# Soft-capped attention and soft mixture of experts on one core: score tiles, chain places and joined tanhs replanned

## The chip, the cores and the metric

The kernel runs on one core of one Trainium2 chip. The metric is device time in microseconds. Before the change the median of three runs is 281.64 us (281.38 to 281.78).

The core's engines work on instruction queues of their own and wait for each other through semaphores: PE (TensorE, matrix products and transposes), DVE (VectorE), ACT (ScalarE), POOL (GpSimd) and SP (SyncE, here only transfers). Each queue is worked off strictly in the order in which the program puts it down.

## The reference

Attention with soft-capped scores over 8 x 12 heads, 448 tokens, head size 64, then a soft mixture of 8 experts with 4 slots each:

```python
scores = scale * np.matmul(q, k.transpose(0, 1, 3, 2))
scores = cap * np.tanh(scores / cap)                       # cap = 30
attn = np.exp(scores - np.max(scores, axis=-1, keepdims=True))
attn = attn / (np.sum(attn, axis=-1, keepdims=True) + 1e-09)
attn_out = np.matmul(attn, v)

logits = x @ phi                                           # x: attn_out as 3584 x 768
d = softmax of logits over the tokens                      # written out in the reference
slot_input = d.T @ x
h = np.maximum(slot_input[e] @ w1[e], 0.0); slot_out[e] = h @ w2[e]
c = softmax of logits over the slots                       # written out in the reference
out = c @ slot_out
```

## The kernel before

**Tiles and chunks.** Two heads make a pair: 48 pairs, two of which share one load (a quad, `Q`, 24 of them, three to a batch element). A score tile is 64 + 64 keys of two heads by 448 queries, that is 128 x 448; a pair has 7 of them, so there are 336. They are worked in 56 chunks of 6 (`CH`), each chunk in two halves of 3 (`CS`). One half of scores fills three PSUM banks.

**What happens to a chunk `j`.**
- PE makes the scores of a half (`qk_chunk`, products on L349).
- ACT takes the tanh of each half out of PSUM (`tanh_chunk`, L366). In a chunk of the tuple `JOINED` one instruction takes both halves (L362), from a six-bank tile (`board`) that replaces the two three-bank tiles from the first joined chunk to the last.
- The exponential follows. `exp_chunk(j)` is one ACT instruction (L374) over the tiles that ACT keeps. The first tiles of the chunks in `SHARED` (chunk: (tiles, buffer)) go to DVE instead, as a *chain* of seven steps (`poly_exp`, L602 to L609) that builds 2^x with a polynomial and integer bit work: steps 0, 1, 3 and 6 are scalar steps (one input tensor), steps 2, 4 and 5 tensor steps (two inputs). All chains share one pair of buffers, `xf` and `xp`.
- ACT runs chunk `j`'s exp between the tanhs of chunk `j + 1` and chunk `j + 2`; the exps of chunks 0 and 1 stand right behind their own tanhs, so chunk 2 has none behind its tanh.
- Two chunks after a pair's last tile, PE multiplies its weights with the values (`pv_first`, `pv_tail`, `pv_rest`; L627) into one PSUM bank (`pv`, the only one of its kind). DVE takes the reciprocal of the row sums (L634, in `norm`) and multiplies (L637, tile `xq`). Only then may the next pair's products go into the bank.

**The order is written out by hand.** The main loop runs over the chunks, and `run(j, slot)` calls, between its fixed steps, what a table `aux` holds for that slot. The slots of a chunk are, in order, `0`, `m` (between the two tanhs), `e`, `a`, `b`, `r`, `c`, `d`; `<` and `>` put a call ahead of or behind the others of a slot. `r` is special: where a pair is finished in the chunk, its calls stand between the reciprocal and the multiplication of `norm`. The dictionary `POLY` says for each (chunk, slot) which steps of which chains go there. `WHEN` places the loads, the transposes of k and q (copied out of PSUM by DVE on L281), the transposes of x (`x_transp`, L689), the logits (`logits`), the slot sums (`slot_sums`, DVE's `slacc` on L778) and so on; `spare`, `fill` and `busy` put filler products on PE.

**Order within a chunk.** Behind the tanhs and the exp, PE's queue has `pv_first`, the calls of `a`, `pv_tail`, the next chunk's first half of scores, the calls of `b`, `pv_rest`, the calls of `c`, the second half of scores, the calls of `d`. In a joined chunk the first half of scores stands behind `pv_rest` instead.

**The end.** In chunk 55 the last pairs are finished outside the loop's pattern (`TAILSEQ`): products of pair 45 in the `pv` bank, then those of pair 46 (`pvm`) and pair 47 (`pvl`) in banks of their own, transposes and logits between them. Behind the attention come the slot sums of the last batch element, the two expert layers (`layer1`, `layer2`) and the output.

Of the kernel before, what the change touches and what calls it, by code (L numbers as in the profile page):

```python
# [37 lines left out]
def kernel(  # L38
# [23 lines left out]
    NQB = H // 4  # L62
# [313 lines left out]
    def exp_chunk(j):  # L376
# [4 lines left out]
    JOINED = (10, 14, 17, 21, 24, 28, 29, 31, 35, 38, 42, 45, 49)  # L381
    SHARED = {1: (2, 0), 3: (3, 0), 4: (3, 0), 6: (2, 0), 7: (3, 0), 9: (3, 0), 11: (3, 0), 12: (3, 0), 14: (3, 0), 16: (3, 0), 18: (3, 0), 19: (3, 0), 21: (3, 0), 23: (3, 0), 25: (3, 0), 26: (3, 0), 28: (3, 0), 30: (3, 0), 32: (3, 0), 33: (3, 0), 35: (3, 0), 37: (3, 0), 39: (3, 0), 40: (3, 0), 42: (3, 0), 44: (3, 0), 46: (3, 0), 47: (2, 0), 48: (2, 0), 49: (3, 0), 51: (2, 0), 52: (1, 0), 53: (3, 0), 54: (1, 0)}
    POLY = {(1, 'm'): ((1, 0),),
            (1, 'e'): ((1, 1),),
            (1, '>a'): ((1, 2),),
            (1, '>b'): ((1, 3),),
            (1, '>d'): ((1, 4),),
            (2, 'r'): ((1, 5),),
            (3, 'e'): ((3, 0),),
            (3, '<a'): ((3, 1), (1, 6)),  # L390
            (3, '<b'): ((3, 2),),
            (3, '>c'): ((3, 3),),
            (4, '<a'): ((3, 4),),
            (4, '>a'): ((3, 5),),
            (4, '<c'): ((4, 0),),
            (5, 'e'): ((4, 1), (3, 6)),
            (5, '<a'): ((4, 2),),
            (5, '>b'): ((4, 3),),
            (5, '>c'): ((4, 4),),
            (6, 'e'): ((6, 0), (4, 5), (6, 1)),  # L400
            (6, '<a'): ((4, 6),),
            (6, '>d'): ((6, 2),),
            (7, 'm'): ((6, 3),),
            (7, 'e'): ((7, 0),),
            (7, '>a'): ((6, 4),),
            (7, '<b'): ((6, 5),),
            (7, '<d'): ((7, 1),),
            (8, '0'): ((7, 2), (7, 3)),
            (8, '>b'): ((6, 6), (7, 4)),
            (8, '>c'): ((7, 5),),  # L410
            (9, 'm'): ((9, 0),),
            (9, '<a'): ((7, 6),),
            (9, '>b'): ((9, 1),),
            (9, '>d'): ((9, 2),),
            (10, 'e'): ((9, 3),),
            (10, '>b'): ((9, 4),),
            (10, '>d'): ((9, 5),),
            (11, 'e'): ((11, 0),),
            (11, '<a'): ((9, 6),),
            (11, '>a'): ((11, 1),),  # L420
            (11, '>b'): ((11, 2),),
            (11, '<c'): ((11, 3),),
            (11, '>c'): ((11, 4),),
            (12, '<a'): ((12, 0),),
            (12, '<b'): ((11, 5),),
            (12, '<c'): ((12, 1),),
            (12, '>d'): ((11, 6),),
            (13, '<b'): ((12, 2),),
            (13, '>b'): ((12, 3),),
            (13, '>c'): ((12, 4),),  # L430
            (13, '>d'): ((12, 5),),
            (14, '<a'): ((14, 0), (12, 6), (14, 1)),
            (14, '<d'): ((14, 2), (14, 3)),
            (15, '>a'): ((14, 4),),
            (15, '>d'): ((14, 5),),
            (16, 'm'): ((14, 6),),
            (16, 'e'): ((16, 0),),
            (16, '<b'): ((16, 1),),
            (16, '>d'): ((16, 2),),
            (17, 'm'): ((16, 3),),  # L440
            (17, '<a'): ((16, 4),),
            (17, '>d'): ((16, 5),),
            (18, 'e'): ((18, 0),),
            (18, '>a'): ((16, 6), (18, 1)),
            (18, '>b'): ((18, 2),),
            (19, '0'): ((18, 3), (18, 4)),
            (19, 'e'): ((18, 5),),
            (19, '<a'): ((19, 0),),
            (19, '<c'): ((18, 6),),
            (19, '>c'): ((19, 1), (19, 2)),  # L450
            (20, '>b'): ((19, 3),),
            (20, '>d'): ((19, 4),),
            (21, '>a'): ((19, 5), (19, 6)),
            (21, '<b'): ((21, 0), (21, 1)),
            (21, '>c'): ((21, 2),),
            (21, '<d'): ((21, 3),),
            (22, '>b'): ((21, 4),),
            (22, '<d'): ((21, 5),),
            (23, 'm'): ((21, 6),),
            (23, '<a'): ((23, 0),),  # L460
            (23, '>a'): ((23, 1),),
            (23, '>d'): ((23, 2),),
            (24, 'e'): ((23, 3), (23, 4)),
            (24, '>d'): ((23, 5),),
            (25, 'm'): ((23, 6),),
            (25, '<a'): ((25, 0), (25, 1)),
            (25, '>b'): ((25, 2),),
            (25, '<c'): ((25, 3),),
            (25, '>d'): ((25, 4),),
            (26, '0'): ((25, 5),),  # L470
            (26, '<b'): ((25, 6),),
            (26, '<c'): ((26, 0),),
            (26, '>d'): ((26, 1),),
            (27, '>a'): ((26, 2),),
            (27, '>b'): ((26, 3), (26, 4)),
            (28, 'e'): ((26, 5), (28, 0)),
            (28, '<a'): ((26, 6),),
            (28, '>b'): ((28, 1),),
            (28, '>c'): ((28, 2),),
            (29, '>a'): ((28, 3),),  # L480
            (29, '<b'): ((28, 4),),
            (29, '>d'): ((28, 5),),
            (30, 'm'): ((28, 6),),
            (30, '>a'): ((30, 0),),
            (30, '>c'): ((30, 1),),
            (31, '0'): ((30, 2),),
            (31, 'm'): ((30, 3),),
            (31, '<b'): ((30, 4),),
            (31, '<c'): ((30, 5),),
            (32, 'e'): ((32, 0),),  # L490
            (32, '<b'): ((30, 6), (32, 1)),
            (32, '>b'): ((32, 2),),
            (32, '<c'): ((32, 3),),
            (32, '>c'): ((32, 4),),
            (33, 'e'): ((33, 0),),
            (33, '<b'): ((32, 5),),
            (33, '<c'): ((33, 1),),
            (34, '0'): ((33, 2),),
            (34, 'e'): ((33, 3),),
            (34, 'r'): ((33, 4),),  # L500
            (34, '<c'): ((32, 6),),
            (35, '0'): ((33, 5),),
            (35, '<a'): ((33, 6),),
            (35, '<b'): ((35, 0),),
            (35, '>b'): ((35, 1),),
            (35, '<c'): ((35, 2),),
            (36, '<a'): ((35, 3),),
            (36, '>a'): ((35, 4),),
            (37, 'm'): ((35, 5), (35, 6)),
            (37, 'e'): ((37, 0),),  # L510
            (37, '<a'): ((37, 1),),
            (38, 'm'): ((37, 2),),
            (38, '>a'): ((37, 3),),
            (38, '>b'): ((37, 4),),
            (38, '>c'): ((37, 5),),
            (39, 'e'): ((37, 6),),
            (39, '>a'): ((39, 0), (39, 1)),
            (39, '>b'): ((39, 2),),
            (39, '<c'): ((39, 3),),
            (39, '>c'): ((39, 4),),  # L520
            (40, 'e'): ((40, 0),),
            (40, '<b'): ((40, 1),),
            (40, '>b'): ((39, 5),),
            (40, '>c'): ((40, 2),),
            (41, '<b'): ((40, 3),),
            (41, 'r'): ((40, 4),),
            (41, '<d'): ((39, 6),),
# [707 lines left out]
```

## Time and profile before

| | |
|---|---|
| runs, median (lowest to highest) | 281.64 us (281.38 to 281.78) |
| span of the profiled execution, first to last instruction | 279.2 us |
| PE, DVE, ACT, POOL busy, share of the span | 88%, 86%, 89%, 51% |
| tanh in halves (L366), all sizes | 87 instructions, 112.9 us |
| tanh joined (L362) | 13 instructions, 33.6 us |
| exp on ACT (L374), all sizes | 58 instructions, 110.7 us |
| the two tensor steps of the chains with one result each (L605, L607) | 34 each, 26.8 and 27.1 us |
| granted TensorE clock, mean | 0.985 |

The profiled execution's span runs from its first to its last instruction; the times of the runs are some 2.4 us above it. A row of the timeline reads: start and duration in us, engine, line, operation, what is written and read, shapes, count; in brackets the idle time ahead of it and what ended it. In the strip of 40 slices, one digit stands for 7 us.

### The profile page before, as it was taken

Reading aid. Unit: us, or ns where it says so; the run is one execution under the profiler, and the core shown is the slowest. Engines: PE = TensorE matmul, PEld = TensorE weight load, DVE = VectorE, ACT = ScalarE, POOL = GpSimd, SP = SyncE. Lnnn points to the kernel's source line nnn. Section 1 sums busy time; section 2 is a strip of 40 time slices with the busy share of each in tenths; the row PEclk is TensorE's granted clock in tenths of the full one; section 3 lists DMA queues with packets and bytes.
Section 4 is the critical chain, followed back from the end, with each engine's and each line's share of the span. In section 5 each row is a group of like instructions: output and inputs, shape, how many; then the busy total and the mean of one; then the engine's idle time right before and its main releaser. Section 6 shows DMA issues by size and latency. Waiting matters only on the chain.

```text
span 279.2 us, 10421 instructions
## 1 busy us (share of the span) xinstructions
PE 247.0 (88%) x4560; PEld 166.6 (60%) x4560; DVE 239.1 (86%) x473; ACT 248.6 (89%) x195; POOL 142.0 (51%) x198
## 2 busy tenths in 40 slices
PE   8898989998999999989999999899999999998720
PEld 7555556756675766566756675657566678553300
DVE  3479999999999999999999999999999997347940
ACT  4999999999999999999999999999999998237720
POOL 8796548662957296728673758375743230200000
PEclk9999999999999999999999999999999999999995
DMA  6999999999999999999999999999999588979997
GB/s 197 277 193 202 219 219 234 229 221 219 224 225 220 219 229 226 225 217 229 223 226 212 213 219 231 218 210 215 231 217 215 117 279 293 367 290 383 434 424 312
DMA packets 57340, 68.08 MB, mean 244 GB/s; under 512 B 4048, under 2 KB 53840, under 8 KB 56784
## 3 DMA queue, kind: packets, MB, share of 16 engines
q0 software_dynamic: 42448, 35.31, 80.0%
q1 hardware_dynamic: 14704, 32.02, 32.6%
q8 instruction: 35, 0.57, 0.7%
q10 hardware_dynamic: 144, 0.10, 0.1%
q14 instruction: 9, 0.07, 0.1%
HBM read 91.72 MB, written 19.27 MB: 398 GB/s over the span
## 4 chain that ended last, share of the span: by engine, by line
ACT 38%; DVE 27%; PE 27%; issue 3%; POOL 1%; ACTq 0%; DVEq 0%
ACT ex L366 15%; ACT ex L374 15%; PE pv L627 8%; ACT ex L362 6%; DVE xq L637 4%; PE sc L349 3%; DVE xp L605 3%; DVE xp L607 3%; DVE ex L608 2%; DVE ex L602 2%; PE so_ps L1098 2%; PE hp L1070 2%; DVE xf L604 2%; DVE ex L609 2%; DVE xp L606 2%
## 5 line engine op out<-in xcount | busy, mean ns | idle before, releaser
L366 ACT ACTIVATE ex<-sc 128x1344 f16<-128x1344 f32 (+1 forms) x87 | 112.9, 1402 | 0.9 <-PE sc L349 0.9
L374 ACT ACTIVATE ex<-ex 128x1344 bf16<-128x1344 f16 (+5 forms) x58 | 110.7, 1916 | 0.1
L627 PE MATMUL pv<-vbd,ex 128*128 128x130 bf16 (+1 forms) x1610 | 94.0, 212 | 7.6 <-POOL vbd L289 3.4
L627 PEld LDWEIGHTS <-ex 128*128 128x128 bf16 (+1 forms) x1680 | 75.6, 101 | 34.9 <-issue 6.2
L289 POOL CAST vbd<-vraw 64x896 bf16<-64x896 f32 x46 | 47.3, 1028 | 57.3 <-PE pv L627 35.7
L349 PE MATMUL sc<-qT,kT 64*64 64x448 bf16 x672 | 66.0, 359 | 6.7 <-ACT ex L366 4.8
L362 ACT ACTIVATE ex<-sc 128x2688 f16<-128x2688 f32 x13 | 33.6, 2586 | 0.0
L349 PEld LDWEIGHTS <-kT 64*64 64x64 bf16 x672 | 22.1, 105 | 16.3 <-ACT ex L366 6.9
L637 DVE TENSOR_TENSOR xq<-pv,rec 128x448 bf16<-128x448 f32 x46 | 28.7, 625 | 1.6
L607 DVE TENSOR_TENSOR xp<-xp,xf 128x1344 f16<-128x1344 f16 (+2 forms) x34 | 27.1, 798 | 0.6
L608 DVE TENSOR_TENSOR ex<-ex,xp 128x1344 uint16<-128x1344 uint16 (+2 forms) x34 | 26.9, 791 | 0.2
L605 DVE TENSOR_TENSOR xp<-xf 128x1344 f16<-128x1344 uint16 (+2 forms) x34 | 26.8, 789 | 0.2
L116 POOL DMA_DIRECT2D w1b<-in_moe_w_dram x32 | 26.3, 825 | 0.0
L602 DVE TENSOR_SCALAR ex<-ex 128x1344 uint16<-128x1344 f16 (+2 forms) x34 | 17.0, 500 | 1.4 <-ACT ex L366 0.8
L606 DVE TENSOR_SCALAR xp<-xp 128x1344 f16<-128x1344 f16 (+2 forms) x34 | 17.2, 505 | 0.6
L281 DVE COPY kT<-kps 128x896 bf16<-128x896 bf16 x23 | 14.2, 617 | 4.0 <-PE kps L276 2.8
L297 POOL MEMSET vbd<- 64x1 bf16 x22 | 2.8, 129 | 28.6 <-PE pv L627 28.3
L604 DVE TENSOR_SCALAR xf<-ex 128x1344 uint16<-128x1344 uint16 (+2 forms) x34 | 16.7, 491 | 0.4
L185 POOL DMA_DIRECT2D qb<-in_q_dram x22 | 16.3, 740 | 1.2 <-PE qps L279 0.5
L609 DVE TENSOR_SCALAR ex<-ex 128x1344 uint16<-128x1344 uint16 (+2 forms) x34 | 16.4, 483 | 0.4
L120 POOL DMA_DIRECT2D w2d<-in_moe_w_dram x21 | 16.4, 816 | 0.0
L185 POOL DMA_DIRECT2D kb<-in_k_dram x22 | 16.3, 739 | 0.0
(124 smaller groups left out, 320.2 us busy)
## 6 DMA issues: line engine op xcount, KB each, us to landing
w1b<-in_moe_w_dram POOLq DMA_DIRECT2D x32, 384.0 KB, 10.2
vraw<-in_v_dram SPq DMA_DIRECT2D x44, 224.0 KB, 6.2
w2d<-in_moe_w_dram POOLq DMA_DIRECT2D x21, 384.0 KB, 9.9
w2t<-w2d SPq DMA_DIRECT2D x21, 384.0 KB, 6.2
qb<-in_q_dram POOLq DMA_DIRECT2D x22, 224.0 KB, 8.2
kb<-in_k_dram POOLq DMA_DIRECT2D x22, 224.0 KB, 8.1
w2b<-in_moe_w_dram POOLq DMA_DIRECT2D x11, 384.0 KB, 9.5
out_dram<-ob SPq DMA_DIRECT2D x2, 1536.0 KB, 7.7
```

The costliest lines, as they stand in the source:

```text
L116: pool.dma_start(out=w1b[e][:, js, fs], in_=w1r[:, e, js, fs])
L185: pool.dma_start(out=t, in_=quad_ap(nm, Q))
L289: pool.tensor_copy(vbds[Q % 2][r, :, :, c0:c0 + DH], raw[r])
L349: ins = pe.matmul(sc[cs, u, 0:S], qkT["k", Q][r, c, cs], qkT["q", Q][r, :, cs], start=True, stop=True).ins
L362: apart["t", i - 1] = apart["t", i] = act.activation(exs[j].bitcast(F16), own["board"][:, :, 0:S], ACT.Tanh, scale=qk_scale / cap).ins
L366: ins = act.activation(exs[j][:, half * CS + u0:half * CS + u1, :].bitcast(F16), (own[0] if i == u0 == 0 else sc)[:, u0:u1, 0:S], ACT.Tanh ...
L374: act.activation(exs[j][:, u0:u1, :], exs[j][:, u0:u1, :].bitcast(F16), ACT.Exp, scale=cap)
L605: lambda: dve.tensor_tensor(p, s, s.bitcast(F16), op=ALU.mult),
L607: lambda: dve.tensor_tensor(p, p, s, op=ALU.mult),
L608: lambda: dve.tensor_tensor(y, y, p, op=ALU.add),
L627: pe.matmul(out_, exs[j][r, u, q0:q0 + (HP if tail else P)], v_, start=(c == 0 and g == gs[0] < NF), stop=(c == NT - 1), skip_group_check= ...
L637: dve.tensor_tensor(xq[Q][:, h, s0:s1, :], pv[:, 0:s1 - s0, 0:DH], rec.to_broadcast([P, s1 - s0, DH]), op=ALU.mult)
```

## The change

Three tables are replaced; no function of the computation changes.

- `JOINED`: 16 chunks instead of 13. Chunks 5, 7, 15 and 51 are new, 14 is out; the six-bank score tile thus serves chunks 5 to 51 instead of 10 to 49.
- `SHARED`: 34 chains in both kernels, but 97 tiles on VectorE instead of 93. The new table has chains in chunks 0 and 2, none in chunk 3; in 22, 24 and 25 (two tiles each) where there were 23 and 25 (three each); three tiles instead of two in chunk 6; and at the end 48, 50, 52, 53, 54 with three tiles each where there were 47, 48, 49, 51, 52, 53, 54 with 2, 2, 3, 2, 1, 3, 1. So ScalarE's exps of these chunks get shorter or longer by as many tiles.
- `POLY`: each step of each chain has a new place. In twelve chunks in which a pair is finished (5, 7, 17, 19, 21, 23, 24, 25, 50, 52, 53, 54) a step now stands in slot `r`; before, slot `r` was used only in chunks without such a pair.
- `WHEN` names each entry for itself instead of once per batch element; the places are the same, and so is the order of all that it places on each engine. The list of quads per batch element is written otherwise.

On PE the six products of the first half of scores move in the chunks that enter or leave `JOINED`; GpSimd's and SyncE's queues hold the same instructions as before.

```diff
-    JOINED = (10, 14, 17, 21, 24, 28, 29, 31, 35, 38, 42, 45, 49)
-    SHARED = {1: (2, 0), 3: (3, 0), 4: (3, 0), 6: (2, 0), 7: (3, 0), ..., 21: (3, 0), 23: (3, 0), 25: (3, 0), 26: (3, 0), ..., 46: (3, 0), 47: (2, 0), 48: (2, 0), 49: (3, 0), 51: (2, 0), 52: (1, 0), 53: (3, 0), 54: (1, 0)}
-    POLY = {(1, 'm'): ((1, 0),),
-            (1, 'e'): ((1, 1),),
-            (1, '>a'): ((1, 2),),
...
-            (52, 'm'): ((51, 3),),
-            (52, 'e'): ((52, 0),),
-            (52, '>a'): ((51, 4),),
-            (52, '>d'): ((52, 1), (51, 5), (52, 2)),
-            (53, 'm'): ((53, 0),),
-            (53, 'e'): ((52, 3), (51, 6)),
-            (53, '<a'): ((52, 4), (53, 1)),
-            (53, '>a'): ((52, 5),),
-            (53, '<c'): ((53, 2),),
-            (53, '>c'): ((52, 6), (53, 3)),
-            (54, '<a'): ((53, 4),),
-            (54, '<b'): ((54, 0), (53, 5)),
-            (54, '>b'): ((54, 1),),
-            (54, '>c'): ((53, 6),),
-            (55, '0'): ((54, 2),),
-            (55, 'e'): ((54, 3),),
-            (55, '<a'): ((54, 4),),
-            (55, '>a'): ((54, 5), (54, 6))}
+    JOINED = (5, 7, 10, 15, 17, 21, 24, 28, 29, 31, 35, 38, 42, 45, 49, 51)
+    SHARED = {0: (2, 0), 1: (2, 0), 2: (3, 0), 4: (3, 0), 6: (3, 0), 7: (3, 0), ..., 21: (3, 0), 22: (2, 0), 24: (2, 0), 25: (2, 0), 26: (3, 0), ..., 46: (3, 0), 48: (3, 0), 50: (3, 0), 52: (3, 0), 53: (3, 0), 54: (3, 0)}
+    POLY = {(0, 'e'): ((0, 0),),
+            (0, '<b'): ((0, 1),),
+            (0, 'r'): ((0, 2), (0, 3)),
+            (0, '<d'): ((0, 4),),
+            (1, 'm'): ((1, 0),),
+            (1, 'e'): ((1, 1), (0, 5), (1, 2)),
+            (1, '<a'): ((0, 6),),
+            (1, '>c'): ((1, 3),),
+            (1, '<d'): ((1, 4),),
+            (2, '>a'): ((1, 5),),
+            (2, '>b'): ((2, 0),),
+            (2, 'r'): ((1, 6), (2, 1)),
...
+            (52, 'e'): ((52, 0),),
+            (52, '<a'): ((52, 1),),
+            (52, '<b'): ((52, 2),),
+            (52, 'r'): ((52, 3),),
+            (53, 'm'): ((52, 4),),
+            (53, '<a'): ((52, 5), (53, 0)),
+            (53, '>a'): ((52, 6),),
+            (53, '>b'): ((53, 1),),
+            (53, 'r'): ((53, 2),),
+            (53, '>c'): ((53, 3),),
+            (54, 'm'): ((54, 0),),
+            (54, '>a'): ((53, 4), (54, 1)),
+            (54, '<b'): ((53, 5),),
+            (54, '>b'): ((54, 2), (53, 6)),
+            (54, 'r'): ((54, 3),),
+            (54, '>c'): ((54, 4),),
+            (54, '>d'): ((54, 5),),
+            (55, '>a'): ((54, 6),)}
```

358 lines of the change are left out of this document (178 added, 180 removed), and 26 rows, old and new, of the table WHEN.

## The prediction

> **What bounds the kernel now.** I read the page first (busy by slice, costliest groups), then ScalarE's timeline for the price of one more instruction, then PE and VectorE where ScalarE's stretch begins and ends.
>
> ```profile
> DVE  3479999999999999999999999999999997347940
> ACT  4999999999999999999999999999999998237720
> L366 ACT ACTIVATE ex<-sc 128x1344 f16<-128x1344 f32 (+1 forms) x87 | 112.9, 1402 | 0.9 <-PE sc L349 0.9
> L627 PE MATMUL pv<-vbd,ex 128*128 128x130 bf16 (+1 forms) x1610 | 94.0, 212 | 7.6 <-POOL vbd L289 3.4
> ```
>
> From slice 2 to slice 33 ScalarE is never idle: its tanh group waited 0.9 us in all, once, at the very start. VectorE stands at 9 as well from slice 4 on, so neither has much to take over. Everything behind slice 33 (expert layers, output) follows the end of the attention and isn't touched.
>
> Durations mislead here, since an instruction starts before the one ahead of it has ended. The price is the distance from start to start:
>
> ```profile
> 206.26 2.03 ACT L374 ACTIVATE ex<-ex 128x1792 bf16<-128x1792 f16 x1
> 208.18 2.48 ACT L366 ACTIVATE ex<-sc 128x1344 f16<-128x1344 f32 x2
> 210.53 1.33 ACT L374 ACTIVATE ex<-ex 128x1344 bf16<-128x1344 f16 x1
> 211.75 2.48 ACT L366 ACTIVATE ex<-sc 128x1344 f16<-128x1344 f32 x2
> 214.09 2.47 ACT L374 ACTIVATE ex<-ex 128x2688 bf16<-128x2688 f16 x1
> 216.42 2.50 ACT L366 ACTIVATE ex<-sc 128x1344 f16<-128x1344 f32 x2
> 218.76 1.74 ACT L374 ACTIVATE ex<-ex 128x1792 bf16<-128x1792 f16 x1
> 220.35 1.34 ACT L366 ACTIVATE ex<-sc 128x1344 f16<-128x1344 f32 x1
> ...
> 222.85 2.14 ACT L374 ACTIVATE ex<-ex 128x2240 bf16<-128x2240 f16 x1
> 224.81 2.54 ACT L366 ACTIVATE ex<-sc 128x1344 f16<-128x1344 f32 x2
> ```
>
> Two half tanhs take 2.34 (208.18 to 210.53), an exp over 3 tiles 1.22, 4 tiles 1.59, 5 tiles 1.96, 6 tiles 2.33: 0.37 us a tile. The exp at 206.26 took 1.92 instead of 1.59: a hidden stall of 0.33, not shown as idle. The rows at 216.42, 220.35 and 224.81 open chunks 52, 53 and 54.
>
> ```profile
> 46.31 2.46 ACT L362 ACTIVATE ex<-sc 128x2688 f16<-128x2688 f32 x1
> 48.60 1.38 ACT L374 ACTIVATE ex<-ex 128x1344 bf16<-128x1344 f16 x1
> ```
>
> A joined tanh takes 2.29, so joining saves 0.05.
>
> **ScalarE's part.** Four tiles leave it (4 x 0.37 = 1.49) and three more tanhs are joined (3 x 0.05 = 0.15): 1.64 us less. Of this only 0.15 lies ahead of chunk 53, because the chunks up to 51 hand over 88 tiles in both kernels; the rest comes from chunk 52 (1 to 3 tiles) and chunk 54 (1 to 3).
> By the Trainium skill, "ScalarE: Activation LUTs", section "What ACT_TABLE_LOAD costs", an instruction has a fixed 186 ns of which back-to-back ones overlap by 93, so three joins would save an estimated 0.28 us. The rows above say 0.05 each, and the sum goes by them.
>
> **The start.** The chunks up to 6 now hand over 13 tiles instead of 10, and chunks 5 and 7 are joined: 3 x 0.37 + 0.10 = 1.2 us less work for ScalarE by chunk 8. Is it kept?
>
> ```profile
> 15.14 4.82 ACT L366 ACTIVATE ex<-sc 128x1344 f16<-128x1344 f32 x4
> ...
> 25.72 2.51 ACT L366 ACTIVATE ex<-sc 128x1344 f16<-128x1344 f32 x2
> ```
>
> ```profile
> 16.14 0.28 PE L879 MATMUL junk<-ones 128*128 128x128 bf16 x2
> 16.34 0.58 PE L279 MATMUL kps<-ident,kb 128*64 128x128 bf16 x14
> 16.86 0.57 PE L349 MATMUL sc<-qT,kT 64*64 64x448 bf16 x6
> ...
> 25.27 0.54 PE L349 MATMUL sc<-qT,kT 64*64 64x448 bf16 x4
> ...
> 28.69 0.90 PE L627 MATMUL pv<-vbd,ex 128*128 128x130 bf16 x15
> ```
>
> ```profile
> 12.14 0.62 DVE L281 COPY kT<-kps 128x896 bf16<-128x896 bf16 x1 [2.81 <-PE kps L276]
> ```
>
> VectorE idles 2.81 us before 12.14, and the first five steps of chunk 0's chain (two tiles, in a row) fit there; they hide behind the wait for kps, and if they ended later, kT and PE would be late by as much. Chunk 0's exp gets 0.75 shorter. But chunk 3's first scores end at 16.86 + 0.57 = 17.43, behind filler and transposes in PE's queue, and the third of the four tanhs (chunk 3's first) starts at 15.14 + 2.34 = 17.48 already now. So ScalarE gets to chunk 3 0.7 earlier and waits. Chunk 5's joined tanh needs its second half's scores too, which end at 25.81, just behind the 25.72 at which the split one starts: 0.1 to 0.2 more. In chunk 5 the next scores move behind the 15 products at 28.69: another 0.1 to 0.3. I count 0.9 of the 1.2 as lost (0.7 to 1.2). Since both kernels have handed over equally much by chunk 51, the loss stays: chunk 53 starts 0.9 - 0.15 later, less stalls like the 0.33 above where they vanish. I take 0.4 us later than now, 220.75 (0.0 to 0.8).
>
> **The end.** VectorE runs in order, and here are its prices and the dates that count.
>
> ```profile
> 222.21 0.51 DVE L602 TENSOR_SCALAR ex<-ex 128x1344 uint16<-128x1344 f16 x1
> 222.63 0.27 DVE L606 TENSOR_SCALAR xp<-xp 128x448 f16<-128x448 f16 x1
> ...
> 225.90 0.38 DVE L778 TENSOR_TENSOR slacc<-slps,slacc 128x224 f32<-128x224 f32 x1
> 226.20 0.26 DVE L609 TENSOR_SCALAR ex<-ex 128x448 uint16<-128x448 uint16 x1
> 226.38 0.50 DVE L606 TENSOR_SCALAR xp<-xp 128x1344 f16<-128x1344 f16 x1
> 226.92 0.86 DVE L607 TENSOR_TENSOR xp<-xp,xf 128x1344 f16<-128x1344 f16 x1
> 227.69 0.27 DVE L602 TENSOR_SCALAR ex<-ex 128x448 uint16<-128x448 f16 x1
> ...
> 228.83 0.20 DVE L634 RECIPROCAL rec<-pv 128x7 f32<-128x7 f32 x1
> 229.07 0.62 DVE L637 TENSOR_TENSOR xq<-pv,rec 128x448 bf16<-128x448 f32 x1
> 229.61 0.61 DVE L689 COPY xT<-xps 128x896 bf16<-128x896 bf16 x1
> ...
> 232.31 0.28 DVE L609 TENSOR_SCALAR ex<-ex 128x448 uint16<-128x448 uint16 x1
> ...
> 232.74 0.62 DVE L637 TENSOR_TENSOR xq<-pv,rec 128x448 bf16<-128x448 f32 x1
> ```
>
> ```profile
> 229.75 0.34 PE L876 MATMUL junk<-ones 128*128 128x384 bf16 x1
> 230.14 0.90 PE L627 MATMUL pv<-vbd,ex 128*128 128x130 bf16 x12
> ...
> 232.25 1.43 PE L627 MATMUL pvm<-vbd,ex 128*128 128x130 bf16 x21
> ...
> 235.29 0.86 PE L627 MATMUL pvl<-vbd,ex 128*128 128x130 bf16 x12
> ```
>
> Start to start, a three-tile scalar step takes 0.42 (222.21 to 222.63), a three-tile tensor step 0.77 (226.92 to 227.69), both 0.12 more if the next step needs the result (226.38 to 226.92 is 0.54). The reciprocal takes 0.24, or 0.12 with another step behind it, xq 0.54, xT the same, slacc 0.30. The one pv bank goes on to PE when xq has been written: 229.07 + 0.62 = 229.69, then filler at 229.75 and the next pair's products at 230.14. From there PE works nearly without a break to the last products. Those on chunk 54 (behind the first six of the 21 at 232.25) need chunk 54's chain, done at 232.59; the next transposes need the xq that ends at 233.36.
>
> Now, the last chains have 3 tiles instead of 1, 3, 1 in chunks 52 to 54. In the new queue chunk 52 does steps 0, 1, 2 and xT ahead of its reciprocal; step 0 needs the first half tanh, which ends 1.38 us into a chunk of 4.67: 1.38 + 0.54 + 0.89 + 0.77 + 0.54 = 4.12, reciprocal, step 3 and xq make 5.20. VectorE is thus free 0.5 us after chunk 53 opens, at 221.25. Then
> - chunk 53: 0.89 + 0.77 + 3 x 0.42 + 0.12 + 0.77 + 0.54 + 0.30 + 0.42 = 5.07, to 226.3;
> - chunk 54 to its xq: 0.42 + 0.77 + 0.42 + 0.77 + 0.77 + 0.42 + 0.12 + 0.42 + 0.62 = 4.73, to 231.05, against 229.69 now: 1.36 late;
> - behind it (xT, steps 4 and 5, a half xT of 0.30, step 6) 0.46 + 0.89 + 0.77 + 0.30 + 0.50 = 2.92: chunk 54's chain ends at 233.97 instead of 232.59, 1.38 late, and the last xq of this row at 234.75 instead of 233.36.
>
> ScalarE meanwhile needs 7.3 us for chunks 53 and 54, VectorE 12: what ScalarE gives up here lands on the queue that PE then waits for. Its own last exp comes about 1 us earlier and waits for nobody. The end moves by 1.4 us. Bounds: 0.3, if chunk 53 opens as early as now, xq42 is 0.3 earlier and each of 30 steps 0.01 cheaper; 2.3, if chunk 53 opens 0.8 late and steps stretch by 4%, as chunk 53's do now.
>
> The profiled span is 279.2, and the median of the runs 281.64, so 2.4 us lie around the span; I add to the median: 281.64 + 1.4 = **283.0 us**, 281.9 to 283.9 by itself.
>
> **In between** the chunks carry the same tiles at other places. Two-tile chains in 22, 24 and 25 stand for three-tile ones in 23 and 25, six tiles both ways. By the prices above no chunk from 9 to 52 ends with VectorE more than 2.7 us behind the opening of the next, so I cost this at nothing; the cover is ScalarE's pace, and without it one step of 0.42 to 0.77 would delay an xq. Data movement is untouched: GpSimd's and SyncE's queues hold the same instructions.
> The Trainium skill ("SBUF — State Buffer", section "SBUF: two separate sides") speaks against the change: VectorE's two-port steps lock a port pair that GpSimd's casts need, for a whole instruction. By it four scalar steps on four more tiles could hold the vbd casts, for which PE waited 3.4 us above, by an estimated 0.3 us at most; the sum leaves it out.
>
> **Rivals.**
> A, faster: VectorE isn't what ends the attention, because PE hands over its sums earlier in the longer chunk 52 or waits elsewhere. Then ScalarE's cut counts, less the start's loss: 281.64 - 1.64 + 0.9 = 280.9, or 280.0 if nothing is lost; 280.5. For it: ScalarE's unbroken 9s. Against it: the 12 us queued into 7.3.
> B, much slower: in twelve chunks (5, 7, 17, 19, 21, 23 to 25, 50, 52 to 54) a chain step now stands between reciprocal and xq, where none did. Each holds the pv bank 0.3 to 0.65 longer, PE starts its next pair later, and its scores come after ScalarE's need. It decides once the delay passes PE's slack; half of 8 x 0.4 ahead of chunk 50 on top of the forecast is 1.6: 284.6. Against it: the step fills a gap in which VectorE itself waits, 0.12 each.
> C, nothing: the late queue costs what the start and the vanished stalls bring, 281.6.
>
> **How the numbers follow.** Forecast 0.54, A 0.23, B 0.11, C 0.12. Less than 0.2%, 0.56 us, can't be told from no change. Faster: A, 0.23. Same: C and a little of the forecast's low end, 0.14. Slower: 0.63. The range leaves out half of B and the lower end of A: 280.4 to 284.3.
>
> **What would show it.** Right: chunk 3 opens near 17.5, ScalarE's idle or stretched pitches grow ahead of chunk 8, VectorE's queue leaves chunk 54 some 5 us after chunk 55's tanh has started, PE is idle for about a microsecond ahead of the products at 230.14, and the last exp is done long before pvl asks for it. Wrong: if that xq ends before 230, the forecast's step on VectorE's queue falls; if ScalarE's starts keep 1.2 us from chunk 8 on, the one on PE's filler falls; if pitches stretch in chunks 17 to 25, B holds.

## The result, and the profile after

The changed kernel takes 293.19 us, median of 4 runs (291.31 to 295.51), against 281.71 (281.38 to 282.24) beside it: ratio 1.0417, interval 1.0363 to 1.0471. The forecast was 283.0 and its range ended at 284.3. The profiled execution spans 291.0 us against 279.2.

The page of the changed kernel: busy tenths by slice with the granted TensorE clock, the share of each engine in the chain that ended last, and two groups with their idle time and what ended it.

```profile
DVE  3888999999999999999999999998899996447840
ACT  3949999999999999999999999999999993236730
PEclk9959999999999999999999999999999997999985
...
DVE 52%; PE 32%; issue 5%; ACT 4%; POOL 3%; ACTq 0%; POOLq 0%; DVEq 0%
...
L366 ACT ACTIVATE ex<-sc 128x1344 f16<-128x1344 f32 (+1 forms) x81 | 102.1, 1312 | 7.5 <-PE sc L349 7.1
L638 PE MATMUL pv<-vbd,ex 128*128 128x130 bf16 (+1 forms) x1610 | 94.2, 213 | 14.7 <-DVE xq L648 9.5
```

The same rows of the page of the kernel before, where they have not been shown:

```profile
PEclk9999999999999999999999999999999999999995
...
ACT 38%; DVE 27%; PE 27%; issue 3%; POOL 1%; ACTq 0%; DVEq 0%
```

ScalarE's tanhs now wait 7.5 us instead of 0.9, PE's products 14.7 instead of 7.6, most of it for VectorE's `xq`. Before, ScalarE made up the largest share of the chain that ended last (38%); now it has 4% and VectorE 52%. The clock has two holes that it had not: slice 3 (14.6 to 21.8 us) and slice 34 (from 240 us on).

Where the 11.83 us of the two spans come in (openings of chunks on ScalarE, read from the two timelines, after minus before):

| | after minus before | gained or lost since the line above | forecast |
|---|---|---|---|
| chunk 3 opens | +4.35 | +4.35 | about 0 |
| chunk 8 opens | +4.14 | -0.21 | |
| chunk 48 opens | +6.38 | +2.24 | 0 |
| chunk 53 opens | +7.59 | +1.21 | +0.4 in all up to here |
| `xq` of pair 44 written | +10.52 | +2.93 | +0.96 |
| last products (`pvl`) begin | +11.83 | +1.31 | 0 |
| end of the span | +11.83 | 0 | 0 |

Chunk 0, ahead of which no edit changes anything, opens 0.35 later in this execution; in the executions of the variants below it opens from 0.33 earlier to 0.60 later. So a few tenths at the start are no effect of an edit.

In this kernel the chain's steps 0 to 6 are L613 and L615 to L620, the reciprocal L645, `xq` L648, the products L638.

**One step, close up.** VectorE's and then GpSimd's timeline of the changed kernel in chunk 7 (start, duration):

```profile
41.17 0.20 DVE L645 RECIPROCAL rec<-pv 128x7 f32<-128x7 f32 x1
41.30 1.22 DVE L613 TENSOR_SCALAR ex<-ex 128x1344 uint16<-128x1344 f16 x1
42.44 0.61 DVE L648 TENSOR_TENSOR xq<-pv,rec 128x448 bf16<-128x448 f32 x1
```

```profile
41.23 0.92 POOL L289 CAST vbd<-vraw 64x896 bf16<-64x896 f32 x1 [3.10 <-issue]
```

The three-tile scalar step took 0.51 at 222.21 in the kernel before; here it takes 1.22. GpSimd's cast of the next values began 0.07 ahead of it and ended at 42.15, and the step ended 0.37 behind that: it stood still until the cast was done. The cast begins here because it waits for the same thing as the reciprocal, the end of a pair's products (the cast at 231.87, shown below, names it: `<-PE pv L638`). `xq`, which reads PSUM, isn't held by casts: here it begins behind one, but in the kernel before 44 of the 46 lay under a cast, and none took more than 0.63. In the old order `xq` stood directly behind the reciprocal and covered most of the cast; the new order puts a step that reads and writes SBUF alone into that place.

Counted in both timelines are the chain steps that begin while a cast runs, more than 0.3 us ahead of its end. Before: 2, of which 1 is stretched, by 0.22 us. After: 18, of which 17 are stretched, by 10.0 us in sum against the undisturbed duration of the same step and shape. Of the 17, 9 stand in slot `r`: 7 of them between the reciprocal and the `xq` of one of the twelve chunks, and 2 in chunk 0, where no pair is finished. The one in each kernel that isn't stretched began within 0.03 us of its cast and had the way first. The Trainium skill ("SBUF — State Buffer", section "SBUF: two separate sides") states this as an exclusive lock of a port pair shared by VectorE and GpSimd, held for a whole instruction, with the loser blocked; the rows agree.

GpSimd's instructions that issue transfers lie over chain steps as well. Steps that lie under these and under no cast take longer than usual by 2.3 us in sum before and by 2.8 after (counting each that is over 0.06 longer), so they don't carry the difference.

**The start.** VectorE, GpSimd, PE and ScalarE in the changed kernel:

```profile
9.76 0.82 DVE L613 TENSOR_SCALAR ex<-ex 128x896 uint16<-128x896 f16 x1
10.62 0.39 DVE L615 TENSOR_SCALAR xf<-ex 128x896 uint16<-128x896 uint16 x1
11.04 1.23 DVE L616 TENSOR_TENSOR xp<-xf 128x896 f16<-128x896 uint16 x1
12.31 1.03 DVE L617 TENSOR_SCALAR xp<-xp 128x896 f16<-128x896 f16 x1
13.38 0.62 DVE L618 TENSOR_TENSOR xp<-xp,xf 128x896 f16<-128x896 f16 x1
14.04 0.62 DVE L281 COPY kT<-kps 128x896 bf16<-128x896 bf16 x1
14.58 0.61 DVE L281 COPY qT<-qps 128x896 bf16<-128x896 bf16 x1
```

```profile
9.40 0.93 POOL L267 CAST casts<-raw 128x896 bf16<-128x896 f32 x1 [0.78 <-DMA raw<-in_q_dram]
10.65 2.44 POOL L289 CAST vbd<-vraw 64x896 bf16<-64x896 f32 x2 [0.31 <-DMA vraw<-in_v_dram]
```

```profile
15.24 0.38 PE L349 MATMUL sc<-qT,kT 64*64 64x448 bf16 x2 [1.85 <-DVE qT L281]
...
17.09 1.32 PE L349 MATMUL sc<-qT,kT 64*64 64x448 bf16 x6
...
20.84 1.33 PE L349 MATMUL sc<-qT,kT 64*64 64x448 bf16 x12
```

```profile
18.46 1.29 ACT L366 ACTIVATE ex<-sc 128x1344 f16<-128x1344 f32 x1 [1.51 <-PE sc L349]
21.84 2.47 ACT L366 ACTIVATE ex<-sc 128x1344 f16<-128x1344 f32 x2 [2.09 <-PE sc L349]
```

The five steps of chunk 0 that were to fit into VectorE's gap (2.81 us ahead of the `kT` copy at 12.14) end at 14.00: the first, third and fourth lie under casts, with 0.82, 1.23 and 1.03 where such steps take 0.38 (15.11), 0.63 (16.48) and 0.40 (113.50) elsewhere in this trace. `kT` comes 1.90 later than before. PE stands 1.85, and the granted clock is 0.50 from 15.99 to 22.82 us: PE takes 1.32 for six scores. The same six in the kernel before:

```profile
14.79 0.76 PE L349 MATMUL sc<-qT,kT 64*64 64x448 bf16 x6
```

The scores of chunk 3, in the last of PE's rows above, begin at 20.84 instead of 16.86, and the chunk opens at 21.84.

**The end.** The steps of chunks 52 to 54 on VectorE, the casts on GpSimd, and PE behind them:

```profile
227.19 1.08 DVE L617 TENSOR_SCALAR xp<-xp 128x1344 f16<-128x1344 f16 x1
...
231.94 1.57 DVE L616 TENSOR_TENSOR xp<-xf 128x1344 f16<-128x1344 uint16 x1
...
237.28 1.49 DVE L616 TENSOR_TENSOR xp<-xf 128x1344 f16<-128x1344 uint16 x1
...
239.60 0.61 DVE L648 TENSOR_TENSOR xq<-pv,rec 128x448 bf16<-128x448 f32 x1
```

```profile
226.96 0.95 POOL L289 CAST vbd<-vraw 64x896 bf16<-64x896 f32 x1
231.87 0.93 POOL L289 CAST vbd<-vraw 64x896 bf16<-64x896 f32 x1 [3.95 <-PE pv L638]
...
237.01 1.05 POOL L289 CAST vbd<-vraw 64x896 bf16<-64x896 f32 x1
```

```profile
240.27 0.34 PE L902 MATMUL junk<-ones 128*128 128x384 bf16 x1 [2.14 <-DVE xq L648]
240.66 0.94 PE L638 MATMUL pv<-vbd,ex 128*128 128x130 bf16 x12
...
243.67 1.84 PE L638 MATMUL pvm<-vbd,ex 128*128 128x130 bf16 x21
...
247.12 0.86 PE L638 MATMUL pvl<-vbd,ex 128*128 128x130 bf16 x12
```

Three of these steps lie under casts: 1.08 instead of 0.50, 1.57 and 1.49 instead of 0.85, together 1.94 us. The forecast had the `xq` of pair 44 fall 0.96 further behind than chunk 53; 0.96 + 1.94 is the 2.9 that is measured. PE then stands 2.14 us, the granted clock is 0.50 from 241.27 to 244.69, and from its filler to `pvl` PE takes 6.85 (240.27 to 247.12) instead of 5.54 (229.75 to 235.29).

### The profile page after: what moved, and what is told of

Same layout as the page of the kernel before. It is cut to its first block, busy times and chain, and to the rows that moved or that the text cites. A ratio compares the mean times of both kernels' runs of the same rounds, so it can differ in the third digit from the quotient of the medians.

```text
span 291.0 us, 10420 instructions
## 1 busy us (share of the span) xinstructions
PE 248.6 (85%) x4560; PEld 169.0 (58%) x4560; DVE 251.7 (86%) x473; ACT 248.5 (85%) x192; POOL 144.5 (50%) x198
## 4 chain that ended last, share of the span: by engine, by line
DVE 52%; PE 32%; issue 5%; ACT 4%; POOL 3%; ACTq 0%; POOLq 0%; DVEq 0%
PE pv L638 9%; DVE xq L648 7%; DVE xp L616 7%; DVE xp L618 5%; DVE ex L619 5%; DVE xf L615 4%; DVE xp L617 4%; PE sc L349 3%; DVE xT L700 3%; DVE ex L613 3%; DVE ex L620 3%; DVE qT L281 3%; DVE kT L281 2%; PE so_ps L1124 2%; POOL vbd L289 2%
## 5 line engine op out<-in xcount | busy, mean ns | idle before, releaser
L366 ACT ACTIVATE ex<-sc 128x1344 f16<-128x1344 f32 (+1 forms) x81 | 102.1, 1312 | 7.5 <-PE sc L349 7.1
L638 PE MATMUL pv<-vbd,ex 128*128 128x130 bf16 (+1 forms) x1610 | 94.2, 213 | 14.7 <-DVE xq L648 9.5
L374 ACT ACTIVATE ex<-ex 128x1344 bf16<-128x1344 f16 (+4 forms) x58 | 103.1, 1782 | 0.1
L638 PEld LDWEIGHTS <-ex 128*128 128x128 bf16 (+1 forms) x1680 | 76.7, 102 | 41.7 <-issue 11.8
L616 DVE TENSOR_TENSOR xp<-xf 128x1344 f16<-128x1344 uint16 (+1 forms) x34 | 30.4, 894 | 0.4
L648 DVE TENSOR_TENSOR xq<-pv,rec 128x448 bf16<-128x448 f32 x46 | 28.6, 621 | 1.2
L619 DVE TENSOR_TENSOR ex<-ex,xp 128x1344 uint16<-128x1344 uint16 (+1 forms) x34 | 27.9, 821 | 0.2
L618 DVE TENSOR_TENSOR xp<-xp,xf 128x1344 f16<-128x1344 f16 (+1 forms) x34 | 27.8, 819 | 0.3
L617 DVE TENSOR_SCALAR xp<-xp 128x1344 f16<-128x1344 f16 (+1 forms) x34 | 20.8, 611 | 0.4
L615 DVE TENSOR_SCALAR xf<-ex 128x1344 uint16<-128x1344 uint16 (+1 forms) x34 | 19.0, 558 | 0.4
L620 DVE TENSOR_SCALAR ex<-ex 128x1344 uint16<-128x1344 uint16 (+1 forms) x34 | 18.3, 538 | 0.4
L613 DVE TENSOR_SCALAR ex<-ex 128x1344 uint16<-128x1344 f16 (+1 forms) x34 | 18.2, 534 | 0.0
L700 DVE COPY xT<-xps 128x896 bf16<-128x896 bf16 (+1 forms) x24 | 14.3, 596 | 2.3 <-PE xps L691 2.3
```

Of the source, the lines that this page charges most:

```text
L366: ins = act.activation(exs[j][:, half * CS + u0:half * CS + u1, :].bitcast(F16), (own[0] if i == u0 == 0 else sc)[:, u0:u1, 0:S], ACT.Tanh ...
L374: act.activation(exs[j][:, u0:u1, :], exs[j][:, u0:u1, :].bitcast(F16), ACT.Exp, scale=cap)
L616: lambda: dve.tensor_tensor(p, s, s.bitcast(F16), op=ALU.mult),
L617: lambda: dve.tensor_scalar(p, p, c3 * 2 ** 24 / STEP ** 2, c1 - 1, ALU.mult, ALU.add),
L618: lambda: dve.tensor_tensor(p, p, s, op=ALU.mult),
L619: lambda: dve.tensor_tensor(y, y, p, op=ALU.add),
```

## The experiments

P is the theory above: chain steps that meet casts stand still, and what PE waits for is late by as much. All medians stand beside runs of the kernel before on the same chip (281.6 to 281.95); "lost" is the difference of the two medians.

### Which part carries the loss

`a_no0`: the changed kernel without chunk 0's chain.

```diff
-    SHARED = {0: (2, 0), 1: (2, 0), 2: (3, 0), ...
-    POLY = {(0, 'e'): ((0, 0),), (0, '<b'): ((0, 1),), (0, 'r'): ((0, 2), (0, 3)), ...
+    SHARED = {1: (2, 0), 2: (3, 0), ...
+    POLY = {(1, 'm'): ((1, 0),), (1, 'e'): ((1, 1), (1, 2)), ...
```

> The changed kernel without the chain in chunk 0 (ScalarE takes all six tiles there, 95 tiles on VectorE). Theory P (VectorE's SBUF steps that meet a GpSimd cast of values stand still until it ends; in chunk 0 they meet it and make qT late, PE idles and its clock drops): the 4.4 us by which chunk 3 opens late go, 293.2 becomes 288 to 289.5. Theory Q (as predicted: chunk 0's chain is hidden, only the number of steps at the end counts): no change, 293 to 294.

288.84 us, ratio 1.0265 (1.0235 to 1.0295). Chunk 3 opens 0.28 earlier than in the kernel before, as chunk 0 does, and the clock has no hole at the start. Of the changed kernel's 293.19 us, 4.4 hang on this chain, as P has it.

`a_oldend`: the changed kernel with the old tables from the chain of chunk 46 on.

```diff
-    SHARED = {..., 46: (3, 0), 48: (3, 0), 50: (3, 0), 52: (3, 0), 53: (3, 0), 54: (3, 0)}
+    SHARED = {..., 46: (3, 0), 47: (2, 0), 48: (2, 0), 49: (3, 0), 51: (2, 0), 52: (1, 0), 53: (3, 0), 54: (1, 0)}
...
```

> The changed kernel with the old table from chain 46 on (14 instead of 15 tiles, old places); chunk 0, the joined chunks and all before 46 stay new. Theory P: what the end loses, 1.4 us in the chunks 48 to 55 and 4 us behind them, goes: 287.5 to 289. Theory Q: the 1.4 us of the forecast go, 291.5 to 292.

288.77 us, ratio 1.0275 (1.0242 to 1.0308): the median is 4.4 below the changed kernel's, as P has it. The profiled execution doesn't put all of that at the end. Its span is 4.5 shorter: 3.0 of that come in at chunk 3, where PE stands 2.02 us for the late `qT` but the clock stays at full speed, and 3.7 behind chunk 53; in between it loses 2.2 more, with the clock at half from 201.45 to 204.86. What the end loses is read more cleanly from `b_end` below.

`a_nor`: in the twelve chunks with a finished pair the step in `r` moves to right behind `xq`.

```diff
-            (7, 'r'): ((7, 0),),
...
+            (7, '<c'): ((7, 0),),
...
```

> The changed kernel with the chain steps of slot r in the 12 chunks that finish a pair put right behind xq instead of ahead of it; the same steps otherwise. Theory P: a cast starts when the pair's products end, just when slot r's step runs; six of these steps are stretched by 3.8 us in all in the profile, so 2 to 4 us go: 289 to 291. Theory Q (a step ahead of xq costs 0.3 to 0.65 of pv bank time whatever GpSimd does, hidden ahead of chunk 50): less than 1 us, above 292.

293.84 us, ratio 1.042 (1.0376 to 1.0463): a miss. Of the moved steps three still meet a cast, by 0.22 each, and others meet one that didn't (14 stretched steps, 7.6 us in sum, in place of 17 and 10.0). The start lost more: chunk 3 opens 4.99 late. Leaving slot `r` isn't enough; what counts is where the casts fall.

`a_all3`: the three edits together.

> The three edits together: no chain in chunk 0, no step ahead of xq, old table from chain 46 on; the joined chunks and the places in between stay new. Theory P: the three causes are all there is, 281 to 283. Theory Q: about 291. If it stays above 284, a fourth cause sits in the joined chunks 5, 7, 15 or in the other places.

287.16 us, ratio 1.0202 (1.0175 to 1.023): a miss, 4 us above the expected range. 11 steps, 5.4 us, still meet casts: 3 in chunks 1 and 2 and 7 in chunks 5 to 44, the part that had been costed at nothing. The clock also falls to half once more, from 44.93 to 48.34 us, and chunk 10 opens 1.9 further behind than chunk 9.

So I went the other way and put single parts of the change into the kernel before.

`b_chain0`: chunk 0's chain alone, at the places of the new table.

```diff
+    SHARED = {0: (2, 0), 1: (2, 0), 3: (3, 0), ...
+    POLY = {(0, 'e'): ((0, 0),), (0, '<b'): ((0, 1),), (0, 'r'): ((0, 2), (0, 3)), (0, '<d'): ((0, 4),), ...
```

> The kernel before with a chain of two tiles in chunk 0 added, its first five steps placed as in the changed kernel, the last two in chunk 1; nothing else. Theory P: qT comes late by the casts that the steps meet, PE idles, its granted clock drops, chunk 3 opens 3 to 4.5 us late: 284.5 to 286. Theory Q: hidden, ScalarE gains 0.75 and loses it at chunk 3: 281.3 to 282.

285.74 us, ratio 1.0135 (1.0111 to 1.016): 3.8 lost. Chunk 3 opens 3.89 later and every later chunk keeps just that, up to 4.10 at chunk 55. Nothing behind it makes good what the first 20 us lose: ScalarE has no idle time left to give.

`b_mid`: the new chains and places of chunks 9 to 44 alone.

```diff
...
-            (23, 'e'): ((23, 0),), ...
+            (21, 'r'): ((21, 1),), (23, 'r'): ((22, 3),), (24, 'r'): ((24, 1),), (25, 'r'): ((24, 6),), ...
```

> The kernel before with the new table for chains 9 to 44 alone (same number of tiles, chunks 22, 24, 25 for 23, 25; old joined chunks, old start and end). Theory P: some seven steps meet a cast, 1.5 to 3 us: 283.2 to 285. Theory Q: nothing, 281.4 to 282.2.

284.10 us, ratio 1.0102 (1.0054 to 1.015): 2.5 lost, with 9 steps stretched by 4.1 us, 7 of them, by 3.5, in chunks 9 to 44.

`b_end`: the new tables from the chain of chunk 46 on.

```diff
-    SHARED = {..., 46: (3, 0), 47: (2, 0), 48: (2, 0), 49: (3, 0), 51: (2, 0), 52: (1, 0), 53: (3, 0), 54: (1, 0)}
+    SHARED = {..., 46: (3, 0), 48: (3, 0), 50: (3, 0), 52: (3, 0), 53: (3, 0), 54: (3, 0)}
...
```

> The kernel before with the new table from chain 46 on alone (15 instead of 14 tiles, three steps ahead of xq in chunks 50, 52, 53 and 54). Theory P: three or four steps meet a cast, the end loses 4 to 5.5 us: 285.5 to 287.5. Theory Q: the 1.4 us of the forecast, 282.5 to 283.5.

287.53 us, ratio 1.021 (1.019 to 1.023): 5.9 lost, at the upper edge of what P gave and far from the rival. 5 steps are stretched by 2.9 us, 4 of them, by 2.5, at the end, and PE stands the same 2.14 us ahead of the last products. The three parts sum to 12.2 us; the whole change lost 11.5. The list of joined chunks and the tables of chunks 1 to 8 are in none of the three, so how near the two come is partly chance.

### Is it the cast?

`b_r_sbuf` and `b_r_psum`: the kernel before with one more VectorE instruction between reciprocal and `xq` in the twelve chunks, a multiplication by one in place; the first over a weight tile in SBUF, the second over the pair's sums in PSUM.

```diff
+    def step(pr):
+        w = w1b[0][:, 0:CS, 0:S]                  # b_r_sbuf
+        p = pv_homes[pr][:, 0:S]                  # b_r_psum
+        dve.tensor_scalar(w, w, 1.0, 0.0, ALU.mult, ALU.add)
...
+    for j in (5, 7, 17, 19, 21, 23, 24, 25, 50, 52, 53, 54):
+        at(j, "r", step, pair_of[j])
```

> The kernel before with one more VectorE step between reciprocal and xq in chunks 5, 7, 17, 19, 21, 23 to 25, 50, 52 to 54: a scalar step from SBUF to SBUF over 3 x 448 bf16 of a loaded weight, times 1 in place (0.42 us alone). Theory P: nearly every one meets the cast that starts when the products end, and takes 1.0 to 1.3 us; 283.5 to 288. Theory Q: each takes 0.42 to 0.5 and it costs what the twin without SBUF costs.

> The twin: the same twelve places, but the step goes over the pv bank in PSUM in place (448 fp32, times 1, about 0.55 us alone). Theory P: it doesn't meet the cast, takes 0.5 to 0.65 each time, and the kernel is at least 1.5 us faster than with the SBUF step: 281.7 to 284. Theory Q: not faster than the SBUF step, rather slower, since the step itself is longer.

292.39 us, ratio 1.0358 (1.03 to 1.0415), and 289.12, ratio 1.0266 (1.0222 to 1.031). The view of that line in the first and in the second kernel (shortest, median and longest in ns):

```profile
L797 DVE TENSOR_SCALAR w1b<-w1b x12: 569/1136/1341, 30.4 to 236.9; 128x1344 bf16<-128x1344 bf16 x12
```

```profile
L797 DVE TENSOR_SCALAR pv<-pv x12: 632/632/633, 29.7 to 234.4; 128x448 f32<-128x448 f32 x12
```

Same place, same chunks: the step in SBUF takes from 0.57 to 1.34, its twin in PSUM 0.63 every time. The nine SBUF steps that began under a cast took 0.71 to 1.34, the three that didn't 0.57 or 0.58; eleven of the twelve PSUM steps lay under a cast and show nothing of it. That settles that the stretching comes from the SBUF side. The medians lie 3.3 us apart, more than P's 1.5, though the intervals meet at 1.03. The levels were missed by both theories: even the undisturbed twin costs 7.2 us for twelve instructions. In chunks 5 and 7 it is hidden (chunk 9 opens no later), by chunk 30 it has cost 3.0, and most of the rest comes behind chunk 53. But the twin also adds 12 x 0.63 = 7.6 us of work to VectorE, which the change doesn't, so what of this is the held pv bank, rival B's cost, and what the longer queue isn't separated.

`a_nocast` and its control `b_nocast`: the changed kernel and the kernel before without the casts of the values.

```diff
     def vcast(Q, n):
-        pool.tensor_copy(vbds[Q % 2][r, :, :, c0:c0 + DH], raw[r])
         if Q != 1:
-            load_v(max(Q + 1, 2), n)
+            raws["v", max(Q + 1, 2)] = vraw
```

> The changed kernel without GpSimd's casts of the values (and without the values' loads from quad 2 on), so that the products run on zeros; all other engines' queues as they are. Theory P (VectorE's steps stand still behind casts, PE then idles and its granted clock falls): no stretched step is left, nearly all of the loss goes, 281.5 to 285. Theory Q (the queue itself is too long at the end, and a step ahead of xq costs by its own length): the loss stays, 288 to 293.

> Control: the kernel before, with the same left out (no casts of the values, no loads of the values from quad 2 on). Both theories: its chain steps hardly meet a cast now, so at most the few waits of PE for vbd go, 280.5 to 282.

286.31 us, ratio 1.0182 (1.0141 to 1.0224), and 283.65, ratio 1.008 (1.0043 to 1.0118). The first lies between the two theories' ranges, 1.3 above P's. The pair is to be compared with each other: 2.7 us remain of the 11.5. The one chain step that is still stretched lies under a cast of q or k, which both kernels keep. The control came out 2 us slower than expected. Part of that is in the last transfer (below); the rest is that chunks 28 to 36 open 0.7 to 1.3 later. It begins with a pause of PE of 1.02 us at 113.79, for which the profile names no releaser, and its cause stays open. Between the two, chunk 53 opens 0.34 later in the changed kernel (forecast: 0.4) and the `xq` of pair 44 comes 1.57 later (forecast: 1.36). Those two dates hold with the casts gone. The last products (`pvl`) then come 2.57 later, where the forecast had 1.4: PE stands 1.58 us ahead of them, and the granted clock is 0.50 from 232.67 to 236.08.

`a_0late`: the changed kernel with chunk 0's chain behind the `kT` and `qT` copies that PE waits for.

```diff
-    POLY = {(0, 'e'): ((0, 0),), (0, '<b'): ((0, 1),), (0, 'r'): ((0, 2), (0, 3)), ...
+    POLY = {(0, '>d'): ((0, 0), (0, 1), (0, 2)), (1, 'm'): ((0, 3),), (1, 'e'): ((0, 4), (1, 0), (0, 5), (1, 1)), ...
```

> The changed kernel with the chain of chunk 0 kept, but its steps put behind the copies kT and qT of quad 1. Theory P: the steps still meet GpSimd's casts and are stretched, but qT is no longer late, PE doesn't idle and its clock stays: chunk 3 opens within 1 us of the kernel before, 288.5 to 290. If the stretched steps themselves are what costs, without qT: above 291.5.

293.23 us, ratio 1.0396 (1.0369 to 1.0423): a miss, though chunk 3 opened 0.25 earlier than in the kernel before, as expected. VectorE's, GpSimd's and PE's timeline tell why:

```profile
16.68 1.13 DVE L612 TENSOR_SCALAR xf<-ex 128x896 uint16<-128x896 uint16 x1
17.73 1.14 DVE L617 TENSOR_SCALAR ex<-ex 128x896 uint16<-128x896 uint16 x1
...
20.40 0.62 DVE L281 COPY kT<-kps 128x896 bf16<-128x896 bf16 x1
```

```profile
16.58 2.04 POOL L289 CAST vbd<-raw 64x896 bf16<-64x896 f32 x2
```

```profile
21.07 0.96 PE L279 MATMUL qps<-ident,qb 128*64 128x128 bf16 x14 [3.65 <-DVE kT L281]
```

Two steps meet the casts of quad 1's values, the next `kT` is late instead, and PE stands 3.65 us. The collision only moved on by one quad.

### The clock behind PE's idle time

In all these runs a late copy and a lower clock came together. `a_fill` keeps the late copy of the changed kernel and fills PE's wait for it with products that nobody uses.

```diff
+    def early(i, n):
+        scores[i] = half_of(i)
+        busy(n, scores[i][:, 0, 0:3 * P])
+
     def qk_chunk(i):
-        scores[i] = half_of(i)
+        if i not in scores:
+            scores[i] = half_of(i)
...
+    at(1, ">a", early, 5, 27)
```

> The changed kernel with 27 filler products more on PE in chunk 1, between the filler that it has and the wait for qT (about 1.5 us of work at full clock), written into the score tile of chunk 2's second half, which is free there. The copies of k and q are as late as before, so the wait stays. Theory P1 (the lower granted clock behind the idle stretch is part of the loss): PE's clock stays at full through 14.5 to 21.8 us, the six scores at 17 us take 0.57 instead of 1.32 us and the twelve at 20.8 us 0.7 or so instead of 1.33, chunk 3 opens about 2 us earlier than in the changed kernel, and the time falls to 291 to 291.8. Theory P2 (the clock only goes along; the late copy is the whole loss): chunk 3 opens within 0.4 us of the changed kernel's, the time within 0.6 of it.

292.83 us, ratio 1.0408 (1.038 to 1.0435). The trace follows P1, the theory of the lower clock: no hole at the start, chunk 3 opens 2.5 us earlier than in the changed kernel, chunk 55 1.7 earlier, and VectorE's last instruction ends 1.6 earlier. The time doesn't show it and lies where P2 has it: behind the last transfer, the span ends 12.4 us after that instruction instead of 10.9, and the changed kernel's own runs spread over 4 us. So I put the same filler beside `b_chain0`, whose runs lie within 1 us.

> The kernel before with chunk 0's chain (285.74 without the filler) and 27 filler products between PE's own filler and the wait for qT. P1 (the lower clock carries about half of this loss): chunk 3 opens 1.2 to 2.2 us later than in the kernel before instead of 3.9, and the time is 283.0 to 284.2. P2 (the clock only goes along): 285.3 to 286.1.

284.10 us, ratio 1.0088 (1.007 to 1.0107): 2.4 lost, where `b_chain0` lost 3.8. PE in `b_chain0` and then with the filler:

```profile
14.29 0.58 PE L349 MATMUL sc<-qT,kT 64*64 64x448 bf16 x2 [1.52 <-DVE qT L281]
14.81 1.46 PE L881 MATMUL junk<-ones 128*128 128x384 bf16 x4
...
16.73 1.32 PE L349 MATMUL sc<-qT,kT 64*64 64x448 bf16 x6
```

```profile
15.25 0.38 PE L354 MATMUL sc<-qT,kT 64*64 64x448 bf16 x2 [0.74 <-DVE qT L281]
15.55 0.82 PE L887 MATMUL junk<-ones 128*128 128x384 bf16 x4
...
16.69 0.76 PE L354 MATMUL sc<-qT,kT 64*64 64x448 bf16 x6
```

With the filler PE gets its operand 0.96 later, and even so its six scores end 0.6 earlier, because they run at full rate; chunk 3 opens 1.88 behind the kernel before instead of 3.89. About half of what chunk 0's chain cost at chunk 3 was the lower clock behind the idle time.

### The list of joined chunks

`b_join16` takes the new list alone into the kernel before, `a_join13` the old list into the changed kernel.

```diff
-    JOINED = (10, 14, 17, 21, 24, 28, 29, 31, 35, 38, 42, 45, 49)
+    JOINED = (5, 7, 10, 15, 17, 21, 24, 28, 29, 31, 35, 38, 42, 45, 49, 51)
```

> The kernel before with the list of joined chunks of the changed kernel alone (chains and their places as before). Theory P (all of the loss is in chain steps that meet GpSimd's casts and in what follows from them): 281.3 to 282.0, no change that can be told, with no more steps stretched than before. Rival (moving the scores behind the products in chunks 5, 7, 15 and 51 makes ScalarE wait there): 282.3 to 283.5, with openings of chunks 6, 8, 16 and 52 later by 0.2 to 0.4 each.

> The changed kernel with the old list of joined chunks. Theory P (the list as such is worth little, its loss on the kernel before came from chunk 5 and chunk 7 standing joined in a stretch where PE had no slack for it): 292.3 to 293.9, no change that can be told, chunks 6 and 8 open within 0.3 of the changed kernel's. Rival (the new list carries a part of the loss here too): 289 to 292, with chunks 6 to 8 opening over 0.8 us earlier.

286.45 us, ratio 1.018 (1.0144 to 1.0216), and 295.48, ratio 1.0499 (1.046 to 1.0539). Both miss P's number, and the rival's too. Alone the list costs 4.7 us; in the profiled execution, 1.8 above the median, chunk 5 opens 2.65 later and chunk 10 6.13. PE in `b_join16`:

```profile
24.74 0.57 PE L349 MATMUL sc<-qT,kT 64*64 64x448 bf16 x6 [1.11 <-ACT ex L366]
25.24 0.94 PE L279 MATMUL kps<-ident,kb 128*64 128x128 bf16 x14
26.12 1.35 PE L627 MATMUL pv<-vbd,ex 128*128 128x130 bf16 x11
```

The six-bank tile can't be written before the tanh ahead of it is done, PE stands 1.11 us, and then its transposes take 0.94 instead of 0.58 (24.02 in the kernel before). In the changed kernel the list carries no loss: with the old one it is 2.3 us slower, with intervals that just touch. So the list is dear with the old split of tiles and not with the new one, and its price alone says nothing on the change.

## Why the prediction was wrong

Slower was right and the size was not: 1.4 us forecast, 11.5 measured.

- **The step that failed** is the sentence on the shared port. It asked whether VectorE would hold GpSimd's casts, put that at an estimated 0.3 us, whose working it doesn't show, and left it out; it took the lock in one direction only and gave no term to what a cast does to a chain step. 17 steps lose 10.0 us so. Before, the trace held one case that could have told it, VectorE's step at 212.49, with GpSimd's cast below it:

```profile
212.49 1.07 DVE L607 TENSOR_TENSOR xp<-xp,xf 128x1344 f16<-128x1344 f16 x1
```

```profile
211.90 0.95 POOL L289 CAST vbd<-vraw 64x896 bf16<-64x896 f32 x1
```

- **The start** (0.4 us by chunk 53): "they hide behind the wait for kps" rests on undisturbed durations and on an empty gap. GpSimd's casts fill that gap. Chunk 3 opens 4.35 late, about half of it through PE's clock (by `b_chain0` and its filler), a term that the sum didn't have.
- **In between, costed at nothing**: 2.2 us. Counting tiles, or how far VectorE ends behind a chunk, doesn't see a step that gets longer by the place where it stands.
- **The end** was right in its mechanism. VectorE's queue, not ScalarE's, sets the last products, and without casts its 1.36 measures 1.57. Short were 1.94 of stretched steps and 1.31 of slower products behind PE's 2.14 us of waiting; the forecast saw the wait (about 1 us) and gave it no price of its own.
- **Rival A** falls. **Rival B** named the place but not the cause: in the changed kernel 7 of the 17 stretched steps stand between reciprocal and `xq`, with 4.6 of the 10.0 us, but they are stretched by casts and not by the pv bank. How much of the 11.5 such steps would cost without casts isn't separated; `a_nocast` bounds it, together with the end, at 2.7.
- **What would show it**: PE's idle time ahead of the products (2.14 us) and a last exp that is done long before `pvl` asks for it (242.34 against 247.12) came true; chunk 3 "near 17.5" failed first and by the most.

What stays open: the 2 us of the `b_nocast` control, which of the middle's stretched steps (3.5 us in `b_mid`, of which 2.5 show) reach ScalarE, and when a pause of PE lowers the clock (below).

No version tried here is faster than the kernel before.

## What to carry to other kernels

Before moving a VectorE instruction, lay GpSimd's casts over its new place: one that works in SBUF and starts under a cast takes the rest of the cast on top, while one that reads PSUM runs through, so put the PSUM reader there. A wait of PE may cost twice, once as a wait and once for the products behind it at half rate; it did so behind 1.52, 1.85 and 2.14 us here, though not behind every wait of that length, so look at the granted clock. Where it does, filler ahead of a late operand takes the second part away. Tables that were made together can't be judged one by one, in either direction.

## What the runs showed of the hardware that was not expected

- A blocked step does most of its work behind the cast: three-tile scalar steps, 0.50 undisturbed, end 0.36 to 0.37 behind it (228.27 against 227.91 at the end, 42.52 against 42.15 in chunk 7), three-tile tensor steps, 0.85 undisturbed, 0.71 (233.51 against 232.80, 238.77 against 238.06). So its length is the cast's remainder plus a fixed piece, and its price can be read off a timeline.
- PE's rate can halve after short pauses: 1.11 us (`b_join16`), 1.52 (`b_chain0`), 1.85 and 2.14 (the changed kernel). The Trainium skill ("TensorE: Matmul & The Clock Gate", section "Part 1: The HAM clock gate (the "warmup" mystery)") gives an idle window of about 3.4 us for it; in these traces much less was enough. But it wasn't enough each time: in the changed kernel the clock stayed at full speed behind five pauses of 1.06 to 1.44 us, the longest of them shown here, and in `a_oldend` behind one of 2.02; there it fell at 201.45, with no pause over 0.75 us in the 60 us ahead of it. So the length of a pause alone doesn't decide it. Wherever it fell behind the first 10 us and ahead of the last 20, in any of the 18 profiled executions, it stood at half for 3.41, 6.83 or 10.24 us.

```profile
138.33 0.85 PE L638 MATMUL pv<-vbd,ex 128*128 128x130 bf16 x12 [1.44 <-DVE xq L648]
```

- Behind VectorE's last instruction only the last output transfer is left. The span ends 10.9 to 11.0 us after that instruction in eleven of the 18 profiled executions, 11.1 to 11.4 in `b_chain0`, `b_end` and `a_oldend`, and 12.2 to 12.4 in `a_fill`, `a_nocast`, `b_nocast` and `b_chain0_fill`, with the same instructions ahead of it. The cause stays open. The last row of VectorE's timeline in the changed kernel (span 291.0) and in `a_fill` (span 290.8):

```profile
276.00 4.09 DVE L1219 TENSOR_SCALAR ob<-op,winv 128x768 f32<-128x768 f32 x4 [0.18 <-PE op L1211]
```

```profile
274.36 4.09 DVE L1225 TENSOR_SCALAR ob<-op,winv 128x768 f32<-128x768 f32 x4 [0.18 <-PE op L1217]
```
